# Tiles 4 to 7 of the first layernorm: from DMA transposes to TensorE transposes with the modulation in the eviction

## The chip, the core and the metric

One core of one Trainium2 chip runs the whole block. The metric is device time in microseconds (us); the kernel before takes 265.88 us (median of three runs, 265.82 to 266.1).

## The reference

S = 2048 rows (16 tiles of 128), D = 448, 16 heads of 28, window 256, bf16 data. Two sublayers follow each other, each with a layernorm, a modulation from the conditioning vector `c`, and a gated residual:

```python
mod = (silu(c) @ w_mod).reshape(..., 6, 1, -1)        # sa, ca, ga, sb, cb, gb
h = layernorm(x) * (1 + ca) + sa
q, k, v = split(h @ wqkv)                             # 16 heads of 28
p = softmax(where(0 <= i - j < 256, q k^T / sqrt(28), -1e9))
x = x + ga * (p v) @ wo
h = layernorm(x) * (1 + cb) + sb
z = gelu(h @ w_in);  z1 = z[:, :896];  z2 = layernorm(z[:, 896:])
x = x + gb * ((z1 * (w_sp @ z2 + b_sp)) @ w_out)      # w_sp is 2048 x 2048
```

## The kernel before

The program is a list of named operations with dependencies, tile rotations and one or more engines that may carry each of them. A stored string, `ORDER`, gives the sequence in which they are emitted: a number is an operation (in order of creation), `.1` picks its second engine, `/3` picks the buffer or PSUM bank. So every engine's queue is fixed in advance, and `Planner.emit` puts a semaphore wait ahead of an operation where one is needed. An engine that waits holds everything behind it in its own queue.

The names that matter here:

- `l1_t` (`ln_stats`, `ln_rs`): statistics of tile t's row on VectorE (DVE; `st` is L609, `ag` L612), `ve` = variance + eps (L616), `rs` = power -1/2 on GpSimd (POOL, L617), and `nm` = -mean*rs (L647, and L621 for the second layernorm, `l2`). `nm` lets the normalized tile `xn` be made as x*rs + nm on DVE, POOL (both L630) or ScalarE (ACT, L660); without it, L631 does (x - mean)*rs. `x2` is the same for the second layernorm.
- `transp_pe`: `tr` multiplies `xn` with an identity on TensorE (PE), and the eviction `hT` (L693 on ACT, L698 on DVE) applies the modulation from PSUM. Blocks 0, 1 and 2 (tiles 0, 1 and 2-3) go this way.
- `transp_dma`: `hx` is a DMA transpose of a tile from the SyncE (SP) queue (L717), and four `hm` operations (`modulate`, L707 or L710) apply the modulation in place for the block's 512 rows. Blocks 3, 4, 5 (tiles 4-7, 8-11, 12-15) go this way.
- `project`: `qk` and `v` matmuls, evicted by `qke` (L817 ACT, L820 DVE) and `ve<t>` (L834 ACT, L837 DVE). Four PSUM banks serve these matmuls from block 1 on.
- Attention by tile: `S`, `SE`, `SC`, `SL` are score matmuls, `E...` the exponentials (ACT, L887), `M...` the masks (POOL, L890), `PV`, then `oq` (L1058), `rec`, `nrm` (L1063), `oT` (L1067), `wo`, `x1` (L1077).
- Second half: `h2T`, `h2q`/`h2m` (transpose and modulation by tiles), `z1`/`z2` matmuls and gelus, the spatial matmuls `G` with `ga`/`gu`, the output matmuls `out` with `fin`. `wsp` are DMA transposes of `w_sp` from the SP queue. `wog` (L871) scales `wo` by the gate. `warm` are filler matmuls at the start.

PE runs in several shapes of its array: whole matmuls (mode 128), 32-row tiles for scores, 32-column tiles for `PV` and what is contiguous with it, and 64-row tiles for the ragged quarter of the contraction (`_r`).

Of the kernel before, what the change touches and what calls it, by code (L numbers as in the profile page):

```python
# [179 lines left out]
1 34 32 31 0 2 3 4 8 11 23 27 22 33 24 25 28 21 29 1693/0 1694 1695 1696 1697 1698 36 35 37/0 1699 1700 1701 15 67 38 1702 39 40/6 41 42 43 26 68 69  # L180
70 71/2 44 45 46 47 48 49 50 51 52 53 54 55 72/0 76/7 56 73 77.1 78/2 79.1 1703 74/4 1704 57.1 75 6 65.1 60.1 7 61.1 5 64.1 1705 1706 1707 1708 1709
12 18 10 9 62.2 125 126 127 63.2 58.2 180 182 128 129 181 95/7 96 85/0 90/1 91 80/2 105/3 81 86 115/6 106 97 98 82 87 88 92 93 99 83 89 94 116 107 117
118 119 108 109 130/2 133/4 134 131/7 183 66 184 1710 84.1 496/0,0 498/1 1711 1712 132.1 150/1 135/0 165/2 140/3 141 136 151 152 59.2 137 153 154 166
138 167 142 168 139 143 144 251 169 110/2 111 100/3 112 113 114 101 102 103 104 145/1 146 147 148 149 155/3 156 157 158 160/0 161 159 162 163 164
497/1,1 501/9 170/2 171 172 173 185 186 188.1/0 187.1/3 189/1 190 192/3 193 194 30.1 247 245 249 246 248 252 250 253 254 120/6 121 122 123 174.1
513/0,1 514/4 517/6 175/2 176 177 13 19 14 494/3 178 179 191.1 255 256/0 124.1 332 225/1 215/0 227 226 218 228 229 520/1,0 523/5 521/7 217 16 17 495
20 260 195/2 198 197 196 199.1 205/1 206 216 219.1 207 208 209.1 330 333 328 334 331 329 335 336 200/3 202 203 201 204 220/2 221 223 222 224 230/0 231
534/0,1 535/5 536/1 232 235/1 237 240/3 241 242 236 210/2 212 243.1 244 233.1 213.1 238.1 234.1 211 214 537/1,0 499 257.1/1 261 502 259.1/3 263
258.1/4 518 515 262 264 503/0 500 278/2 323/3 337 267 324 279 265 325 266 326 338 540 541 239.1 504/0 505 538 342.1/3 339.1/0 506.1/0 340.1/2 327 281
280 282 542/1,0 543/0 546/3 341.2/4 268/3 269 288/1 290 270 271 303/2 304 516/0 524 522 519 549/0,1 550/0 551/4 291.1 306.1 415 413 411 412 272.1 414  # L190
525/0 305 289 308/3 526 292.1 417 307.1 273/0 274 275 276 277 309 311 552/0,1 553 555 298/1 547/2 560/0 561 544/1 548 539 557 545 283/2 300 286 285
284 287 299 310 312 301 527/1 507/2 416 528/1 418 558 587/1,0 588/2 589/3 302.1 419 554 559 529/2 556 562 569/0 293/3 296 508/1 509 294 510 295 511
297 530 531 590/1,0 591 420 566/0 532 564 565 563 567 568 570 571/1 512 572/2 573/1 907 908 906 905 533 578/0 574 593 595/2,1 599/0 575 576 936 577
579 346 343 345 344 347.1 376/0 348.1 349.1 378 379 350.1 377 380.1 594 592 580.1/0 596/4 602/1,0 603/5 938 361/1 362 363 364 365.1 581/2 381/0 384
383 382 385.1 605/1,2 366/1 368 367 369 370.1 597/2 600/1 598 613/0 614 610 604/4 606 607 608 601 609 640/0,1 642/0 641/1 611 582/1 583 612 940 941
# [12 lines left out]
790/0 791 785/1 786 787 788 789 792/1 815/0 817/0,2 818 1433 1436 810 820 474/0 475 477 476 478.1 931/1 852/0,1 854/5 853/2 825/0 823 822 826 1035/2
1036 1037 793/1 935 794/3 795 934 819 824 821 827 834/0 796 797 798 835 932 933 1038 1043.1 970/0 971 974/2 972/1 973 855/0,1 858 856 1052/0 1053 1054
1069/3 1071 1039/2 1070 1040 1041 1072 1077.1 1042 1044 982 984 986 988 1055 1060.1 857 836.1/0 859 837/2 860/0,1 1090/3 1056/1 1091 1092 830/0 833  # L210
489/2 490 491 1057 1058 831 864/3 865/4 861/2 866 862/1 863 1093 1095.1 492.1 493.1 1059 1061.1 867/0,1 868/1 975 978.1 828 829 832 843/0 838/3 839
840 841 1086/1 1087 1088 842 987 985 989 983 990 991 869/3 1073/0 1074 1089 1076 1094.1 870/2,0 873 1430 1434 1438 871 1096/0 844 980 845/0 979 1075
846/2 1078 981.1 992 995/2 996 999.1/1 993.1/0 1000 994 1295/6 1305/7 1296 1307 1306 1300/3 1297 1301 1154/0 1150 1302 1330/1 1332 1333 1298 1303 1304
1153 1308 1309 1157 847/2 848 1005 1156 849 1155 850 851 1006 1007 1331 1151 1152 1103/1 1104 1158/2 872 874 879/0 1107/2 1340/7 876 880 875 878 877
1109 1097 1008 1009 887/0 1160 1335/4 1337 1110 1338 1343 1106 1334 1299 1079/1 997/2 888 1010 1011 1098 1080 1081 1159 998 1014/1 889.1/0 1015 1315/1
885/0 1105 1108 1112.1 1111.1 1336 1339 882 883 1317 1320/6 1012.2/0 1013 881 1316 1321 884 1310/0 1312 886 1453 1451 1441 1440 1445 1442 890/2 896/0
897 1082 1161 1162 898/0 1083 1120/0 1342 1124 1322 1325/3 1127 1318 1319 1313 1123 1323 1328 891/0 892 1341 893 894 895 1125 1290/1 1126 1326 1344
1324 1121 1122 1291 1311 1128/3 1002.2 1314 1004.1 1084 1163 1099 899/0 900/0 901 902 1292 1020 1001 903 904 1164 1085 1370/7 1180/0 1181 1327 1375/6
1371 1182 1003.2 1045/1 1329 1365/0 1376 1366 1184 1186 1185 1293 1294 1368 1373 1378 1187 1183 1188/2 1372 1367 1380/3 1350/1 1381 1369 1377 1374
1379 1382 1355/2 1199/0 1357 1195 1197 1285/0 1286 1356 1200 1165/1 1169 1172 1198 1383 1288 1353 1358 1202 1168 1170 1196 1201 1171 1021 1016 1022  # L220
1017.2 1100 1130 1023 1024 1129 1101 1025 1131 1026 1029.2/0 1384 1027.1/2 1102 1132 1133 1046 1047 1048 1049 1028 1134 1190 1189 1191 1359 1203/0
1167 1352 1287 1166 1345/3 1360/2 1214/0 1215 1210 1216 1212 1351 1173/3 1289 1354 1211 1361 1225/1 1229 1019.1 1050 1018.1 1348 1217 1363 1228 1051
1192 1205 1030 1455 1034.2 1213 1232 1218/1 1227 1362 1226 1032.1 1031.1 1385/0 1230 1347 1364 1033.1 1259/0 1193 1175 1204 1174 1219 1194 1176 1177
1220 1178 1179 1206 1221 1222 1207 1208 1223 1255 1346 1349 1231 1257 1260 1233/2 1386 1387 1395/2 1397 1390/3 1391 1135/1 1139 1062/3 1064 1235 1224
1209 1063 1065 1066 1388 1389 1142 1393 1138 1258 1262 1392 1394 1261 1256 1137 1405/1 1141 1410/0 1140 1136 1143/1 1412 1400/3 1401 1407 1396 1411
# [72 lines left out]
def bass_adaLN_cond__sliding_block__mixer_gmlp__prompt_kernel(  # L298
# [14 lines left out]
    FH = 896  # L313
# [300 lines left out]
    def ln_rs(name, prio, slot, t0, n, deps, nm):  # L614
# [4 lines left out]
        if not nm:  # L619
            return r  # L620
# [19 lines left out]
    def ln1(b, pr):  # L640
# [8 lines left out]
        for t in range(t0, t0 + n):  # L649
# [12 lines left out]
            if b:  # L662
                opts += [("pool", pool2_ns(512), f_p)] + ([("act", act_ns(512), f_a)])
# [640 lines left out]
```

## Time and profile before

| | |
|---|---|
| median of three runs | 265.88 us |
| profiled execution | 265.4 us, of which 263.7 us are the span from the first to the last instruction |
| granted TensorE clock | 1.000 |
| busy: PE, DVE, ACT, POOL | 257.2, 164.3, 128.8, 95.2 us |
| DMA transposes of `xn` and `x2` tiles | 28, issued from SP |
| mean busy share of the 16 DMA engines by q1 | 40.0% |

A row of a timeline gives start, length, engine, line, operation and tile, the count of instructions merged into it, and in brackets idle time of the engine with what ended it. A row of the chain of waits gives start, length and what. A row of windows gives for each engine busy time and count of instructions. A row of groups ends with busy time in total and the mean in ns, then the idle time before.

### The profile page before, as it was taken

What the parts mean: (1) busy time and instruction counts of PE and PEld (TensorE: products, weight loads), DVE (VectorE), ACT (ScalarE), POOL (GpSimd) and SP (SyncE); (2) the same over time, 40 slices, a digit from 0 to 9 for tenths busy, and PEclk for the clock granted to TensorE, in tenths of its full rate; (3) what the DMA queues carried; (4) which work ended last, traced back from release to release, by engine and by line L of the source; (5) the groups of instructions that cost most, each with busy time, mean ns of one, the idle gap of its engine ahead of it and who ended that gap; (6) DMA issues with size and microseconds to landing.
All of it is one profiled execution on the core that took longest, in us unless ns stands there. A gap on an engine that the chain in (4) does not pass through costs nothing.

```text
span 263.7 us, 7760 instructions
## 1 busy us (share of the span) xinstructions
PE 257.2 (98%) x3395; PEld 128.7 (49%) x3395; DVE 164.3 (62%) x387; ACT 128.8 (49%) x183; POOL 95.2 (36%) x148
## 2 busy tenths in 40 slices
PE   6999999999999999999999999999999999999996
PEld 2675455655455554543434444444444444444453
DVE  4798988788989997979587702352514213344453
ACT  4899999999999999778888000000000000000000
POOL 3594968878878776515331300000000000000000
DMA  6975560256994764768899400000000000000043
GB/s 225 357 193 120 145 163 5 62 125 145 227 114 118 118 87 101 85 130 154 144 199 222 92 2 0 0 0 2 0 0 0 2 0 0 0 2 17 0 142 119
DMA packets 61022, 23.86 MB, mean 91 GB/s; under 512 B 49854, under 2 KB 60861, under 8 KB 60989
## 3 DMA queue, kind: packets, MB, share of 16 engines
q1 hardware_dynamic: 60715, 22.92, 40.0%
q8 instruction: 26, 0.43, 0.6%
q10 hardware_dynamic: 274, 0.46, 0.5%
q14 instruction: 7, 0.06, 0.1%
HBM read 9.47 MB, written 1.84 MB: 43 GB/s over the span
## 4 chain that ended last, share of the span: by engine, by line
PE 91%; DVE 3%; POOL 2%; ACT 1%; DMA 1%; issue 1%; SPq 0%; DVEq 0%; POOLq 0%
PE ps L467 80%; PE ps L464 11%; DVE hT L707 1%; DMA hT<-xn 1%; ACT arena L887 1%; POOL xn L630 1%; POOL arena L890 0%; ACT WQK L734 0%; DVE x_sb L1077 0%; SPq L717 0%; DVE QKT L820 0%; ACT hT L693 0%; PE ps L779 0%; DVE xn L630 0%; DVE o_sb L1063 0%
## 5 line engine op out<-in xcount | busy, mean ns | idle before, releaser
L887 ACT ACTIVATE arena<-ps 128x1024 bf16<-128x1024 f32 x76 | 72.4, 1028 | 2.0 <-PE ps L467 1.4
L1212 DVE TENSOR_TENSOR tmpg<-ps,bsp_bc 128x512 bf16<-128x512 f32 x28 | 19.2, 689 | 60.2 <-PE ps L467 59.9
L467 PE MATMUL ps<-QKT,z 128*128 128x512 bf16 x224 | 52.1, 379 | 0.0
L890 POOL TENSOR_SCALAR_AFFINE_SELECT arena<-arena 128x512 f32<-128x512 f32 x60 | 39.1, 669 | 12.2 <-ACT arena L887 9.5
L467 PEld LDWEIGHTS ps<-QKT,z 128*128 128x128 bf16 x224 | 21.9, 98 | 26.4
L617 POOL TENSOR_TENSOR rs_all<-ve_all,neghalf 128x1 f32<-128x1 f32 (+2 forms) x27 | 18.9, 703 | 33.1 <-DVE ve_all L616 32.9
L467 PE MATMUL ps<-w_spD,z 128*128 128x512 bf16 x112 | 27.9, 379 | 0.0
L467 PE MATMUL ps<-w_spC,z 128*128 128x512 bf16 x112 | 27.8, 379 | 0.0
L467 PE MATMUL ps<-hT,w_in_sb 128*128 128x512 bf16 (+1 forms) x97 | 25.3, 380 | 0.0
L467 PE MATMUL ps<-w_in_sb,hT 128*128 128x448 bf16 (+1 forms) x102 | 24.6, 353 | 0.0
L467 PE MATMUL ps<-w_out_sb,z1T 128*128 128x448 bf16 (+2 forms) x119 | 22.0, 341 | 0.0
L609 DVE BATCH_NORM_STATS2 st_all<-z2raw 128x6 f32<-128x448 bf16 x32 | 18.7, 616 | 4.9 <-ACT z2raw L1135 3.9
L467 PE MATMUL ps<-hT,WQK 128*128 128x128 bf16 (+4 forms) x124 | 19.9, 291 | 0.1
L609 DVE BATCH_NORM_STATS2 st_all<-x_sb 128x6 f32<-128x448 bf16 x32 | 18.6, 608 | 0.0
L467 PE MATMUL ps<-QKT 28*64 28x64 bf16 (+3 forms) x944 | 17.7, 210 | 0.6 <-ACT arena L887 0.3
L1154 ACT ACTIVATE z1T<-ps 128x512 bf16<-128x512 f32 x28 | 15.9, 597 | 4.3 <-PE ps L467 4.2
L467 PE MATMUL ps<-arena,Vaug 128*32 128x128 bf16 x720 | 17.7, 221 | 0.0
L467 PEld LDWEIGHTS ps<-w_spC,z 128*128 128x128 bf16 x112 | 11.0, 98 | 13.2
L467 PEld LDWEIGHTS ps<-w_spD,z 128*128 128x128 bf16 x112 | 11.0, 98 | 13.0
L467 PEld LDWEIGHTS ps<-QKT 28*128 28x128 bf16 (+1 forms) x944 | 11.3, 97 | 11.7 <-ACT arena L887 5.9
L630 POOL TENSOR_SCALAR xn<-x_sb,rs_all,nm_all 128x512 bf16<-128x512 bf16 x20 | 15.4, 781 | 4.0 <-DVE nm_all L647 1.7
L467 PEld LDWEIGHTS ps<-w_out_sb,z1T 128*128 128x128 bf16 x119 | 11.6, 98 | 10.1
(93 smaller groups left out, 331.7 us busy)
## 6 DMA issues: line engine op xcount, KB each, us to landing
wmod_sb<-in_w_mod_dram SPq DMA_DIRECT2D x8, 224.0 KB, 3.8
w_in_sb<-in_B_w_in_dram SPq DMA_DIRECT2D x8, 224.0 KB, 4.0
out_dram<-fin SPq DMA_DIRECT2D x16, 112.0 KB, 1.7
x_sb<-in_A_x_dram SPq DMA_DIRECT2D x3, 448.0 KB, 8.1
bsp_bc<-in_B_b_sp_dram SPq DMA_DIRECT2D x1, 512.0 KB, 4.0
wqk_raw<-in_A_wqkv_dram SPq DMA_DIRECT2D x1, 452.0 KB, 5.7
wmod_sb<-in_w_mod_dram SPq DMA_DIRECT2D x1, 448.0 KB, 4.9
wmod_sb<-in_w_mod_dram ACTq DMA_DIRECT2D x1, 448.0 KB, 5.0
```

What stands on the lines that cost most here:

```text
L464: last = e.matmul(out_[32 * j:32 * j + 32], lhsT=lhsT[:, 32 * j:32 * j + 32], rhs=rhs, start=st, stop=sp, tile_position=(0, 32 * j), **kw)
L467: return e.matmul(out_, lhsT=lhsT, rhs=rhs, start=st, stop=sp, **kw)
L609: st = [dve("%sst%d" % (name, i), prio, dve_ns(D), lambda e, i=i, s_=s_: e.bn_stats(st_all[:, slot, t, i, :], s_()), deps, tens) for i, s_ ...
L617: r = pool(name + "rs", prio, 420 + 148 * n, lambda e: e.tensor_tensor(rs_all[:, slot, t0:t1], ve_all[:, slot, t0:t1], neghalf[:, t0:t1], ...
L630: return e.tensor_scalar(dst, src, rs_all[:, slot, t:t + 1], nm_all[:, slot, t:t + 1], ALU.mult, ALU.add)
L707: return e.tensor_scalar(hT[:, c_, cols], hT[:, c_, cols], modT[:, base_col + 4 + c_:base_col + 5 + c_], modT[:, base_col + c_:base_col + ...
L887: return P.op(name, pr, [("act", 925, lambda e: e.activation(e_out(), e_in(), ACT.Exp, scale=SCALE))], [s_op, t_exp0], tens + [pt], table= ...
L890: return pool(name, pr, pool_ns(n), lambda e: e.affine_select(out=pt32(slot_out.slot, off, dims), in_=pt32(slot_in.slot, off, dims), patte ...
L1154: g = P.op("z1g%d_%d" % (tb, ft), pr - 19, [("act", act_ns(512), lambda e: e.activation(z1T[:, ft, tb * 512:(tb + 1) * 512], ps[:, ten.slo ...
L1212: a = dve("ga%d_%d" % (tb, ft), pr, dve_ns(512), lambda e, tb=tb, ten=ten, tg=tg: e.tensor_tensor(tmpg[:, tg.slot, :], ps[:, ten.slot, :], ...
```

## The change

Block 3 is made by `transp_pe`, with one PSUM bank for each of the four 128-row chunks of h: `tr3_u_i` (chunk u, tile i) are 16 matmuls of 128 columns, and `hT3_u` are four evictions of 128x512 that modulate. The four `hx` and four `hm` of tiles 4 to 7 are gone. All ten `nm` operations are dropped and with them the ACT form of `xn` and `x2`; all normalizations use mean and rs. `ve` may run on POOL.

```diff
-    'by_pe': (1, 1, 1, 0, 0, 0),
+    'by_pe': (1, 1, 1, 1, 0, 0),
...
-    def ln_rs(name, prio, slot, t0, n, deps, nm):
+    def ln_rs(name, prio, slot, t0, n, deps):
         t1 = t0 + n
-        v = dve(name + "ve", prio, 75, lambda e: e.tensor_scalar(ve_all[:, slot, t0:t1], mv_all[:, slot, t0:t1, 1], EPS, None, ALU.add), deps)
-        r = pool(name + "rs", prio, 420 + 148 * n, lambda e: e.tensor_tensor(
+        def ve_fn(e):
+            return e.tensor_scalar(ve_all[:, slot, t0:t1], mv_all[:, slot, t0:t1, 1], EPS, None, ALU.add)
+        v = P.op(name + "ve", prio, [("dve", 75, ve_fn), ("pool", 110, ve_fn)], deps)
+        return pool(name + "rs", prio, 420 + 148 * n, lambda e: e.tensor_tensor(
             rs_all[:, slot, t0:t1], ve_all[:, slot, t0:t1], neghalf[:, t0:t1], ALU.pow), [v, t_nh])
-        if not nm:
-            return r
-        return dve(name + "nm", prio, 75, lambda e: e.scalar_tensor_tensor(
-            nm_all[:, slot, t0:t1], mv_all[:, slot, t0:t1, 0], -1.0, rs_all[:, slot, t0:t1], ALU.mult, ALU.mult), [r])
...
-    def norm(e, slot, t, dst, src, nm):
-        if nm:
-            return e.tensor_scalar(dst, src, rs_all[:, slot, t:t + 1], nm_all[:, slot, t:t + 1], ALU.mult, ALU.add)
+    def norm(e, slot, t, dst, src):
         return e.tensor_scalar(dst, src, mv_all[:, slot, t, 0:1], rs_all[:, slot, t:t + 1], ALU.subtract, ALU.mult)
...
-            opts = [("dve", dve4_ns(512), f_d)]
-            if b:
-                opts += [("pool", pool2_ns(512), f_p)] + ([("act", act_ns(512), f_a)])
+            def f_n(e, t=t, ten=ten):
+                return norm(e, 0, t, xnv(xn, ten.slot), spread(x_sb[:, t, :]))
+            opts = [("dve", dve4_ns(512), f_n)] + ([("pool", pool2_ns(512), f_n)] if b else [])
...
-        per = 1 if b == 0 and n == 1 else 2
+        per = 1 if b == 0 and n == 1 or n == 4 else 2
```

`ORDER` is new from end to end. Read by the names of the operations it stands for, it differs from the one before in this:

- Start. The loads of `wqk` come ahead of tiles 2-3 on SP, tiles 8-11 and `wmodG` ahead of `wo`. `xn1` goes from DVE to POOL; the statistics of tile 1 come ahead of one `hT0` eviction, those of tiles 2-3 behind three copies of `wqk`. `gateA` stands two `v` matmuls earlier.
- Tiles 4 to 7. `l1_4ve`, `l1_4rs`, then `xn6`, `xn5`, `xn4`, `xn7` stand on POOL behind `zv`, `M1_0`, `M0_0` and `M0_1` (before: `xn4` on DVE, the others between the masks). On PE, `tr3_0`, `tr3_1`, `tr3_3` stand between the last `qk2` matmuls and `SE2_1`, `tr3_2` after `v7_0`. `hT3_0`, `hT3_3`, `hT3_2` are on DVE, the last behind `oq0`; `hT3_1` is on ACT.
- Elsewhere. `nrm0`, `nrm3`, `nrm9`, `nrm14` go from POOL to DVE, `xn10`, `xn15`, `x2_12`, `x2_15` from ACT to POOL, `x2_3`, `x2_8`, `x2_11`, `x2_14` from DVE to POOL, `x2_1` and `xn2` from POOL to DVE, most `ve` of the layernorms to POOL. `x1_9` moves behind `oT10`. On SP, `wsp2_6`, which waits for all `PV`, stands ahead of `h2T13` and `h2T12`. The `G` and `out` groups come in another sequence with the same last tile.
- PE has 908 operations instead of 892, and changes its array shape 122 times instead of 117 (counted along the two orders).

More of the change, by code (lines that the diff above doesn't have):

```diff
@@ L184 @@
[L184 to L195, printed above, removed]
@@ L236 @@
[L236 to L238 removed]
+1 2 0 3 4 25 28 21 26 1695/0 1696 1697 1698 1699 1700 1701 32 36 35 34 67 68 69 15 31 22 27 70 37/2 1702 1703 1704 1705 71/0 74/1 33 38 40/3 41 42 43
+39 44 45 46 47 48 49 50 51 52 53 54 55 24 23 56 75.1 62.2 8 125 126 127.1 128 72/4 73 1706 1707 76/2 78/7 79 1708 1709 1710 77.1 63.1 6 60.1 7 5 11 58
@@ new lines @@
+575/0 572 574 571 573 570 585/0 580/1 581 602/2,1 582 943 944 583 584 600 601 606/0 607/1 428 384/0 386 385 387 388.1 586 587/1 603/4 604/2 608
+609/1,0 610/5 369/1 370 371 372 373.1 389/0 611/4 390 392 391 588/1 393.1 612/1,2 613 374/1 375 377 376 378.1 620/0 617 605 615 947 948 945 946 621
+647/0,1 618 589/1 590 591 614 592 619 327/3 329 364/2 366 593 616 622 629/0 328 365 367.1 330.1 649/1 648/0 430.1/3 1427 434 650/1,0 432.1/2 431.1/1
+429.1/4 433 435 368.1 331.1 630 631.1/1 653 651 654 929/0 404/1 405 406 930 407 408.1 931 932 933 655/2,0 656/3 934 935 949 936 937 950 951.1 652
@@ L239 @@
+1686/4 1678/1 1571 1567 1687 1513 1679 1680/4 1681 1682/7 1683 1688/7 1689 1690/5 1691/5 1692 1693 1694
 """
@@ L643, in ln1 @@
         if b == 0:
-            r = [ln_rs("l1_%d" % (t0 + i), pr, 0, t0 + i, 1, [ags[i]], False) for i in range(n)]
+            rs = [ln_rs("l1_%d" % (t0 + i), pr, 0, t0 + i, 1, [ags[i]]) for i in range(n)]
         else:
-            r = [ln_rs("l1_%d" % t0, pr, 0, t0, n, ags, False)]
-        rs = r if b == 0 else [dve("l1_%dnm" % t0, pr, 75, lambda e: e.scalar_tensor_tensor(
-            nm_all[:, 0, t0:t0 + n], mv_all[:, 0, t0:t0 + n, 0], -1.0, rs_all[:, 0, t0:t0 + n], ALU.mult, ALU.mult), r)] * n
+            rs = [ln_rs("l1_%d" % t0, pr, 0, t0, n, ags)] * n
         for t in range(t0, t0 + n):
@@ L651, in ln1 @@
             xn_ten[t] = ten
-            def f_d(e, t=t, ten=ten):
-                return norm(e, 0, t, xnv(xn, ten.slot), spread(x_sb[:, t, :]), False)
-            def f_p(e, t=t, ten=ten):
-                return norm(e, 0, t, xnv(xn, ten.slot), spread(x_sb[:, t, :]), True)
-            def f_a(e, t=t, ten=ten):
-                return e.activation(xnv(xn, ten.slot), spread(x_sb[:, t, :]), ACT.Identity, bias=nm_all[:, 0, t:t + 1], scale=rs_all[:, 0, t:t + 1])
-            opts = [("dve", dve4_ns(512), f_d)]
-            if b:
-                opts += [("pool", pool2_ns(512), f_p)] + ([("act", act_ns(512), f_a)])
+            def f_n(e, t=t, ten=ten):
+                return norm(e, 0, t, xnv(xn, ten.slot), spread(x_sb[:, t, :]))
+            opts = [("dve", dve4_ns(512), f_n)] + ([("pool", pool2_ns(512), f_n)] if b else [])
             xn_op[t] = P.op("xn%d" % t, pr + 0.1, opts, [rs[t - t0]], [ten], port=True)
@@ L1089, in bass_adaLN_cond__sliding_block__mixer_gmlp__prompt_kernel, with f_n @@
         ags = [ln_stats("l2_%d" % j, pr, 1, j, [lambda j=j: x_sb[:, j, :]], [x1_op[j]]) for j in js]
-        rs = ln_rs("l2_%d" % j0, pr, 1, j0, n, ags, True)
+        rs = ln_rs("l2_%d" % j0, pr, 1, j0, n, ags)
         for j in js:
             x2t = Ten(rot("x2", NX2))
-            x2 = P.op("x2_%d" % j, pr, [("pool", pool2_ns(512), lambda e, j=j, x2t=x2t: norm(e, 1, j, xnv(xn2, x2t.slot), spread(x_sb[:, j, :]), True)),
-                                        ("dve", dve4_ns(512), lambda e, j=j, x2t=x2t: norm(e, 1, j, xnv(xn2, x2t.slot), spread(x_sb[:, j, :]), True)),
-                                        ("act", act_ns(512), lambda e, j=j, x2t=x2t: e.activation(
-                                            xnv(xn2, x2t.slot), spread(x_sb[:, j, :]), ACT.Identity, bias=nm_all[:, 1, j:j + 1], scale=rs_all[:, 1, j:j + 1]))],
-                      [rs], [x2t], port=True)
+            def f_n(e, j=j, x2t=x2t):
+                return norm(e, 1, j, xnv(xn2, x2t.slot), spread(x_sb[:, j, :]))
+            x2 = P.op("x2_%d" % j, pr, [("pool", pool2_ns(512), f_n), ("dve", dve4_ns(512), f_n)], [rs], [x2t], port=True)
             h2_raw[j] = P.op("h2T%d" % j, pr, [("sp", 1250, lambda e, j=j, x2t=x2t: e.dma_start_transpose(
```

104 lines of the change are left out of this document (54 added, 50 removed).

## The prediction

> **What bounds the kernel now.** I read the page's busy line first, then the windows by stage, the chain of waits, and PE's timeline wherever the windows show it idle. The profiled execution took 265.4 us, 1.7 more than its span of 263.7 and 0.5 under the median of 265.88; I work out differences against that execution and add them to the median.
>
> ```profile
> PE 257.2 (98%) x3395; PEld 128.7 (49%) x3395; DVE 164.3 (62%) x387; ACT 128.8 (49%) x183; POOL 95.2 (36%) x148
> ```
>
> PE is busy for 98% of the span, no other engine for more than 62%. So the time is PE's own work plus the few holes in it, and an edit counts by what it does to one of these two. The windows (us of each engine, count in brackets, in the order PE, PEld, DVE, ACT, POOL, then granted clock, DMA share, GB/s) say where the holes are:
>
> ```profile
> 12.80:25.00 12.20, 12.20 (x184) 8.31 (x188) 10.96 (x30) 12.03 (x26) 8.71 (x12) 1.00 0.61 150
> 25.00:28.30 3.30, 2.80 (x112) 1.32 (x102) 3.11 (x8) 2.81 (x5) 1.95 (x3) 1.00 0.88 258
> 28.30:73.60 45.30, 45.30 (x1268) 25.18 (x1262) 38.92 (x84) 43.29 (x50) 37.16 (x53) 1.00 0.53 123
> 73.60:86.00 12.40, 11.77 (x370) 6.56 (x366) 11.06 (x27) 12.29 (x14) 10.24 (x15) 1.00 0.70 102
> ```
>
> From 12.8 to 86 us PE is idle in two places only: 0.50 us at 25 to 28.3 and 0.63 us at 73.6 to 86. The clock is granted in full, so none of this is throttling. The chain of waits (start, length, what) shows whose hole the first is:
>
> ```profile
> 12.78 5.91 PE ps L467 x84
> 18.68 1.50 POOL xn L630 x2
> 20.19 1.19 POOL arena L890 x2
> 21.38 0.94 SPq L717
> 22.36 2.60 DMA hT<-xn
> 25.16 1.74 DVE hT L707 x4
> ...
> 112.42 148.67 PE ps L467 x729
> ```
>
> For 8 us the chain leaves PE: POOL makes the normalized tiles 4 to 7, SP issues their DMA transposes, the last lands at about 25, and DVE modulates them in four operations of 1.74 us. That is the path the change replaces. It looks like 8 us to win; but PE had other work meanwhile (12.20 busy of 12.20 before 25). Only what PE actually waits for can be won. PE's timeline there:
>
> ```profile
> 24.81 0.44 PE L467 MATMUL ps<-arena,Vaug 128*32 128x128 bf16 x16
> 25.62 0.40 PE L464 MATMUL ps<-hT,WQK 128*32 128x512 bf16 x4 [0.37 <-DVE hT L707]
> 25.85 0.55 PE L464 MATMUL ps<-wv_sb,hT 128*32 128x448 bf16 x8
> 26.23 0.39 PE L464 MATMUL ps<-hT,WQK 128*32 128x512 bf16 x4
> 26.44 0.86 PE L464 MATMUL ps<-wv_sb,hT 128*32 128x448 bf16 x8
> 27.14 0.60 PE L464 MATMUL ps<-hT,WQK 128*32 128x512 bf16 x8
> ```
>
> Because matmuls are pipelined I count from start to start. The first wait for `hT` shows as 0.37 with DVE's L707 as releaser. The second is hidden in the counts: eight `v` matmuls take 0.38 (25.85 to 26.23) and then 0.70 (26.44 to 27.14), so 0.32 more. The last chunk's modulation was late for both. After 112.42 the chain is PE alone to the end, in one piece of 148.67 us, so nothing that is won or lost after that on another engine counts unless it opens a hole there.
>
> **PE's own work.** The change adds 16 transposes. The identity matmuls of the other blocks are in the trace:
>
> ```profile
> 15.35 0.61 PE L467 MATMUL ps<-ident,xn 128*128 128x128 bf16 x8
> 15.80 0.92 PE L467 MATMUL ps<-wv_sb,hT 128*128 128x448 bf16 x4
> ```
>
> Eight take 0.45 from start to the next start, 0.056 each: 16 cost **+0.9**. Their duration is longer, as the row of their group says (busy in total, mean ns of one):
>
> ```profile
> L467 PE MATMUL ps<-ident,xn 128*128 128x128 bf16 x16 | 1.5, 219 | 0.1
> ```
>
> 219 ns is the latency of one; eight of them in 0.45 us are pipelined, and PE's queue pays 0.056. The Trainium skill ("TensorE: Matmul & The Clock Gate", Part 4: PE-mode transpose) says otherwise of the price: about 275 ns for a 128x128 transpose in a kernel's context, dominated by access latency, with a copy out of PSUM after it; 16 of those would be 4.4 us. The trace's row has the latency near it, but shows that it overlaps; I go by the row, and take the other reading as rival C, in the row's own numbers.
>
> PE also changes its array shape 122 times instead of 117. A change's price comes from two stretches of the same kind, a run of `PV` and then a score shape:
>
> ```profile
> 46.04 0.53 PE L467 MATMUL ps<-arena,Vaug 128*32 128x128 bf16 x24
> 46.50 0.40 PE L467 MATMUL ps<-QKT 28*128 28x64 bf16 x16
> ```
>
> ```profile
> 80.06 0.87 PE L467 MATMUL ps<-arena,Vaug 128*32 128x128 bf16 x48
> 80.87 0.40 PE L467 MATMUL ps<-QKT 28*128 28x64 bf16 x16
> ```
>
> 24 take 0.46, 48 take 0.81: 0.0146 for one, and 0.11 left that does not grow with the count. Five changes: **+0.55** (between 0, if they hide in waits, and 0.55). The same 0.0146 prices the first hole above: 16 `PV` should take 0.23, and 24.81 to 25.62 is 0.81, so 0.58 lost; with the 0.32 the hole is 0.9.
>
> **The hole at 25.** With the transposes on PE, `hT3` comes straight from PSUM. The four SP issues (0.94 for the last), the 2.60 of the landing and the four in-place modulations leave the path; in their place stand `xn` on POOL as before, 0.9 of PE and four evictions, three on DVE, one on ACT. The path gets about 3 us shorter, and the wait goes: **-0.9**. What is late next is the evictions themselves. No row shows a 128x512 eviction with modulation; the nearest are these (busy, mean ns):
>
> ```profile
> L820 DVE CAST QKT<-ps 128x512 bf16<-128x512 f32 x18 | 12.3, 681 | 2.7 <-PE ps L464 2.0 <-PE ps L467 0.2
> ...
> L707 DVE TENSOR_SCALAR hT<-hT,modT 128x512 bf16<-128x512 bf16 x10 | 3.9, 429 | 0.5 <-DMA hT<-xn 0.5
> ...
> L1063 DVE TENSOR_TENSOR o_sb<-oq,rec_all 128x448 bf16<-128x448 f32 x9 | 6.7, 748 | 0.1
> ```
>
> I take 0.68, the cast from PSUM, not the 0.43 of the in-place form; a price of 0.43 would take 0.75 off rival B. The one eviction on ACT and the four `xn` on POOL leave those two engines about as loaded as they were.
>
> **The head.** Before, DVE normalizes tile 1 itself and then evicts `hT1`, for which PE's `qk1` waits until 12.78:
>
> ```profile
> 10.93 0.41 DVE L631 TENSOR_SCALAR xn<-x_sb,mv_all,rs_all 128x512 bf16<-128x512 bf16 x1
> 11.26 0.17 DVE L612 BATCH_NORM_AGGREGATE mv_all<-st_all 128x2 f32<-128x6 f32 x1
> ...
> 12.00 0.72 DVE L698 TENSOR_SCALAR hT<-ps,modT 128x128 bf16<-128x128 f32 x2
> ```
>
> In the new order `xn1` is POOL's, and of the 1.07 us between 10.93 and 12.00 only two aggregates of 0.17 stay ahead of the eviction. So 0.75 can go, if the statistics of tiles 2-3, which now stand ahead of it, do not wait for their load: I take **-0.75**, between 0 and -1.0. Part of it comes back. `wog` does not move with its queue, since it needs `wo`, whose load the new order puts later on SP:
>
> ```profile
> 18.60 2.00 DVE L871 TENSOR_TENSOR wo_sb<-wo_sb,ps 128x1792 bf16<-128x1792 bf16 x1
> 20.52 0.75 DVE L820 CAST QKT<-ps 128x256 bf16<-128x256 f32 x2
> ```
>
> Behind its 2.00 us stand the evictions `qke2` as before (0.75 for two); PE, arriving 0.75 earlier, finds the four `project` banks still full. I take **+0.3**, between 0 and 0.75.
>
> **The rest.** Ten `nm` go, most `ve` of the layernorms go to POOL, ACT loses four operations, `x1_9` moves behind `oT10`. In the 73.6 to 86 window this can relieve at most the 0.63 of holes; one of them is this wait for DVE:
>
> ```profile
> 85.56 0.94 PE L464 MATMUL ps<-wo_sb,oT 128*32 128x448 bf16 x16 [0.18 <-DVE oT L1067]
> ```
>
> I take **-0.3**, between +0.3 (another order has other small holes) and -0.6. `ve` on POOL has no row; it delays `rs` on the same queue by about what DVE's now takes, and what follows it (`xn` a stage ahead of its transposes) has slack, so nothing; without that slack, some 0.1 for each tile. The four `hx` leave SP's queue, and the loads and DMA transposes behind them start earlier; `wsp2_6` ahead of `h2T13` and `h2T12` holds these two until the last `PV`, and I cost that at nothing because PE then has the projections of earlier tiles to do. If this cover fails, a transpose of about 2.6 (the landing above) stands open. The new sequence of `G` and `out` has the same matmuls: nothing.
>
> **Sum.** +0.9 +0.55 -0.9 -0.75 +0.3 -0.3 = **-0.2**: 265.2 for an execution like the one profiled, **265.7** as median. By the skill's price for transposes (4.4 in place of 0.9) the sum would be +3.3.
>
> **The rivals.** *A, faster: the holes close and nothing comes back.* The head gives its whole 1.0, `wog` delays nobody, the 0.63 goes: 0.9 + 0.55 - 0.9 - 1.0 - 0.6 = -1.05, **264.8**. For it: DVE loses `nm` and the in-place `hm`, and the chain's 8 us detour disappears. Against it: DVE was 10.96 of 12.20 busy in just that stage.
>
> *B, slower: DVE becomes the bound between 13 and 28 us.* It has 1.24 + 0.19 = 1.43 us free there. Added are three evictions of 0.68, `nrm0` and `nrm3` of 0.75, `xn2` of 0.41: 3.95; four `hm` (1.74) and two `xn` of some 0.33 from start to start leave: 2.40. Net +1.55. DVE's free time is mostly waiting for PE's results, so not usable; where less than a tenth of it is, PE waits for banks for the whole 1.55 instead of the sum's 0.3, and the holes later stay as they are: -0.2 + 1.25 + 0.3 = +1.35, **267.2**. It decides when the `hT3` and `qke` evictions queue on DVE so that PE, in order, stands behind a full bank; the +0.9 and +0.55 on PE are then paid with nothing to set against them. For it: the windows. Against it: `nrm` has no early reader, and POOL and ACT share the evictions.
>
> *C, transposes at their latency.* If the 16 do not pipeline because each chunk waits for its tile, each costs 0.219 and not 0.056: +2.6, **268.3**. The eight in 0.45 us speak against it.
>
> *D, the replaced path did not matter.* If the wait at 25 goes to another producer (`E`, the scores' masks, `v`), 0.9 is not won, and the time is 266.6; this lies between the forecast and B, and I count it with B.
>
> **How the numbers follow.** A measurement of this kernel can tell about 0.2%, 0.5 us, from no change. Forecast 0.40, with its own range of 265.1 to 266.2, from 0.6 less (the rest's -0.6 and a smaller price of shape changes) to 0.5 more (the head's bound); A 0.27; B with D 0.29; C 0.04. Of the forecast 0.12 lies below 265.35 and 0.28 within 0.2%. Faster: 0.27 + 0.12 = 0.39. Slower: 0.29 + 0.04 = 0.33. Within: 0.28. The range goes from a little under A, 264.5, to B, 267.3; left out are C, and the ends of A and B where holes other than those costed open or close, together under 0.2.
>
> **What would show it.** Right: identity matmuls x32 in place of x16 in their group, 24 DMA transposes of `xn` and `x2` tiles in place of 28, `qk1` starting at about 12.0 in place of 12.78, no idle PE at 25 to 28 released by L707, and PE busy about 1.4 longer in total with 1.6 less of holes. B would show as idle PE at 18 to 30 released by L820, L698 or L871, with DVE over 95% in that window; C as identity matmuls apart from each other with idle time before them. I am wrong in kind if PE's busy time grows by more than 2, or if a hole of over 1 us stands after 30 us where none was before: then an order's later parts, which I cost at nothing, decide.

## The result and the profile after

The changed kernel takes 287.99 us (median of four runs, 287.62 to 288.92) against 265.88: 8.35% more, ratio 1.0835 with a 95% interval of 1.0806 to 1.0864. The forecast was 265.7, and its range ended at 267.3. Ratios further down are to runs of the kernel before taken beside each experiment (median 265.4 to 265.8), with a 95% interval in brackets. The busy line and the windows that answer to those of before:

```profile
PE 262.6 (92%) x3345; PEld 132.2 (46%) x3366; DVE 168.2 (59%) x363; ACT 126.8 (44%) x178; POOL 137.1 (48%) x167
```

```profile
12.80:25.00 12.20, 12.20 (x157) 8.76 (x157) 10.60 (x26) 11.48 (x24) 8.75 (x11) 0.87 0.68 163
25.00:28.30 3.30, 1.68 (x12) 0.70 (x10) 1.24 (x6) 1.52 (x3) 3.30 (x3) 1.00 0.01 2
28.30:73.60 45.30, 36.67 (x949) 20.24 (x953) 33.46 (x62) 31.99 (x37) 43.71 (x48) 0.92 0.24 48
73.60:86.00 12.40, 11.51 (x276) 6.33 (x274) 8.44 (x16) 9.10 (x10) 8.91 (x11) 0.86 0.49 117
```

Only one engine has become busier by much: POOL, from 95.2 to 137.1 us, and from 25 to 73.6 it works almost without a break (3.30 of 3.30, 43.71 of 45.30) while PE, DVE and ACT all have gaps. The number behind POOL's bracket is the granted clock: it fell to 0.86 to 0.92 in three of these stretches. PE is busy for 262.6 us, 5.0 more than with the same queue and a clock of 1.0 in the mult-add kernel below (257.6); how much of the 22 us the lower clock accounts for was not separated. Which work of POOL it is stands in the chain of waits:

```profile
22.05 1.02 POOL rs_all L618
23.17 8.26 POOL xn L626 x4
31.63 0.60 POOL arena L875
32.23 1.02 POOL rs_all L618
33.37 4.13 POOL xn L626 x2
37.50 1.24 POOL arena L875 x2
38.74 4.12 POOL xn L626 x2
42.85 1.24 POOL arena L875 x2
```

For 22 us without a break the chain is POOL, and most of it is `xn`: four tiles take 8.26 us. The chain of before had two of them in 1.50. PE's timeline shows what that does to the new transposes:

```profile
26.23 0.22 PE L466 MATMUL ps<-ident,xn 128*128 128x128 bf16 x1
27.37 0.23 PE L466 MATMUL ps<-ident,xn 128*128 128x128 bf16 x1 [0.93 <-POOL xn L626]
29.43 0.23 PE L466 MATMUL ps<-ident,xn 128*128 128x128 bf16 x1 [1.82 <-POOL xn L626]
31.48 0.29 PE L466 MATMUL ps<-ident,xn 128*128 128x128 bf16 x1 [1.82 <-POOL xn L626]
```

PE transposes a tile, then waits about 2 us for the next. The group rows of the normalization on POOL, after and then before (the last two numbers ahead of the bar's end are busy time and mean ns of one):

```profile
L626 POOL TENSOR_SCALAR xn<-x_sb,mv_all,rs_all 128x512 bf16<-128x512 bf16 x28 | 58.1, 2084 | 0.6
```

```profile
L630 POOL TENSOR_SCALAR xn<-x_sb,rs_all,nm_all 128x512 bf16<-128x512 bf16 x20 | 15.4, 781 | 4.0 <-DVE nm_all L647 1.7 <-DMA hT<-xn 1.3 <-DVE nm_all L621 1.0
```

Same engine, operation, shape and types; 2084 ns against 781. What differs is the arithmetic, x * rs + nm before and (x - mean) * rs after, and where one scalar comes from.

### The profile page after: what moved, and what is told of

Read it like the earlier page. It is cut to its first block, busy times and chain, and to the rows that moved or that the text cites. A ratio compares the mean times of both kernels' runs of the same rounds, so it can differ in the third digit from the quotient of the medians.

```text
span 285.7 us, 7668 instructions
## 1 busy us (share of the span) xinstructions
PE 262.6 (92%) x3345; PEld 132.2 (46%) x3366; DVE 168.2 (59%) x363; ACT 126.8 (44%) x178; POOL 137.1 (48%) x167
## 4 chain that ended last, share of the span: by engine, by line
PE 61%; POOL 20%; ACT 6%; DVE 5%; DMA 3%; issue 3%; SPq 0%; DVEq 0%; POOLq 0%
PE ps L466 57%; POOL xn L626 13%; ACT arena L872 5%; PE ps L463 4%; POOL arena L875 4%; DMA x_sb<-in_A_x_dram 2%; POOL rs_all L618 2%; DVE o_sb L1048 2%; DMA hT<-xn 1%; DVE st_all L608 1%; DVE x_sb L1062 1%; DVE z L626 1%; POOL ve_all L616 1%; POOL hT L692 1%; DVE hT L692 0%
## 5 line engine op out<-in xcount | busy, mean ns | idle before, releaser
L626 POOL TENSOR_SCALAR xn<-x_sb,mv_all,rs_all 128x512 bf16<-128x512 bf16 x28 | 58.1, 2084 | 0.6
L466 PE MATMUL ps<-w_in_sb,hT 128*128 128x448 bf16 (+1 forms) x109 | 26.5, 353 | 1.1 <-ACT z2raw L1118 0.5
L618 POOL TENSOR_TENSOR rs_all<-ve_all,neghalf 128x1 f32<-128x1 f32 (+2 forms) x27 | 19.8, 740 | 10.6 <-DVE ve_all L616 9.8
L466 PE MATMUL ps<-hT,w_in_sb 128*128 128x512 bf16 (+1 forms) x94 | 24.3, 380 | 0.2
L466 PE MATMUL ps<-w_out_sb,z1T 128*128 128x448 bf16 (+2 forms) x119 | 22.8, 341 | 0.0
L466 PE MATMUL ps<-arena,Vaug 128*32 128x128 bf16 x720 | 18.6, 229 | 1.7 <-POOL arena L875 1.0
L466 PE MATMUL ps<-QKT 28*64 28x64 bf16 (+3 forms) x944 | 18.5, 214 | 0.8 <-issue 0.8
L466 PEld LDWEIGHTS ps<-arena,Vaug 128*32 128x32 bf16 x720 | 14.2, 100 | 8.9 <-POOL arena L875 1.5
L463 PE MATMUL ps<-hT,WQK 128*32 128x512 bf16 x208 | 16.0, 395 | 2.2 <-DVE oq L1043 2.2
L1217 DVE TENSOR_TENSOR fin<-ps,x_sb 128x448 bf16<-128x448 f32 (+2 forms) x17 | 9.6, 593 | 12.9 <-PE ps L466 12.1
```

Of the source, the lines that this page charges most:

```text
L463: last = e.matmul(out_[32 * j:32 * j + 32], lhsT=lhsT[:, 32 * j:32 * j + 32], rhs=rhs, start=st, stop=sp, tile_position=(0, 32 * j), **kw)
L466: return e.matmul(out_, lhsT=lhsT, rhs=rhs, start=st, stop=sp, **kw)
L618: return pool(name + "rs", prio, 420 + 148 * n, lambda e: e.tensor_tensor(rs_all[:, slot, t0:t1], ve_all[:, slot, t0:t1], neghalf[:, t0:t1 ...
L626: return e.tensor_scalar(dst, src, mv_all[:, slot, t, 0:1], rs_all[:, slot, t:t + 1], ALU.subtract, ALU.mult)
L1217: fs.append(dve("fin%s%d" % (nm, t), pr, dve_ns(c1 - c0), lambda e, t=t, ten=ten, ft_=ft_, c0=c0, c1=c1: e.tensor_tensor(fin[:, ft_.slot, ...
```

## The experiments

**What makes POOL slow.** The first kernel changes nothing but the pair of operations on POOL.

```diff
         return e.tensor_scalar(dst, src, mv_all[:, slot, t, 0:1], rs_all[:, slot, t:t + 1], ALU.subtract, ALU.mult)
 
+    def norm_p(e, slot, t, dst, src):
+        return e.tensor_scalar(dst, src, rs_all[:, slot, t:t + 1], mv_all[:, slot, t, 0:1], ALU.mult, ALU.add)
+
...
-            opts = [("dve", dve4_ns(512), f_n)] + ([("pool", pool2_ns(512), f_n)] if b else [])
+            def f_p(e, t=t, ten=ten):
+                return norm_p(e, 0, t, xnv(xn, ten.slot), spread(x_sb[:, t, :]))
+            opts = [("dve", dve4_ns(512), f_n)] + ([("pool", pool2_ns(512), f_p)] if b else [])
```

`x2` gets its `f_p` in the same way.

> The changed kernel; only the arithmetic of xn and x2 on GpSimd is altered, from (x - mean) * rs to x * rs + mean: same operands in the other order, another pair of operations. (So the values differ from the reference's.) Order, waits and counts are those of the changed kernel. Theory S (the pair subtract, multiply is what GpSimd takes 2084 ns for): its 28 instructions fall to about 781 ns, the row of before, GpSimd's busy time falls by 28 x 1.3 = 36 us to about 101, and the time to 265.7, between 264.5 and 267.3, the prediction's own figures. Rival P (the operand, a mean read out of the interleaved statistics, or traffic with VectorE makes it slow): the 28 stay at about 2084 and the time at 288. Rival O (the new order is slow by itself): the 28 fall, and the time stays above 275.

Measured: 268.02 us, ratio to before 1.0088 (1.0065 to 1.0112), and the clock back at 1.0. That is 20 of the 22 us, but 0.7 above the range that was expected. Rival O is out as the cause of these 20 us, since this is the new order. The next keeps the operands where the change has them and replaces `ALU.subtract` by `ALU.add`; a third has `ALU.mult, ALU.subtract`.

> The changed kernel with (x + mean) * rs on GpSimd (values differ from the reference's): the scalars stand in the changed kernel's order, and only subtract has become add. If subtract alone is the slow part: 28 instructions at about 781 ns and the same time as with x * rs + mean, within 0.3%. If it is the order of the two steps, the multiplication last: 2084 ns and about 288 us.

> The changed kernel with x * rs - mean on GpSimd (values differ from the reference's): subtract, but as the second step. If any subtract on GpSimd is slow: 28 at about 2084 ns and 288 us. If only subtract as the first step is: 770 to 780 ns and 267.5 to 268.5 us.

Measured: 268.43 us (1.0118, 1.0067 to 1.0169) with add, 288.86 us (two runs; 1.0869, 1.0833 to 1.0904) with the subtract as second step. The group rows on POOL, in the order mult-add, add-mult, mult-subtract:

```profile
L629 POOL TENSOR_SCALAR xn<-x_sb,rs_all,mv_all 128x512 bf16<-128x512 bf16 x28 | 21.3, 770 | 0.6
```

```profile
L629 POOL TENSOR_SCALAR xn<-x_sb,mv_all,rs_all 128x512 bf16<-128x512 bf16 x28 | 21.4, 773 | 0.7
```

```profile
L629 POOL TENSOR_SCALAR xn<-x_sb,rs_all,mv_all 128x512 bf16<-128x512 bf16 x28 | 58.7, 2106 | 0.6
```

The mean out of the interleaved statistics is read in all three, so the operand (rival P) is not it; a subtract in either place is slow. The other way round, in the kernel before:

```diff
             def f_p(e, t=t, ten=ten):
-                return norm(e, 0, t, xnv(xn, ten.slot), spread(x_sb[:, t, :]), True)
+                return norm(e, 0, t, xnv(xn, ten.slot), spread(x_sb[:, t, :]), False)
...
-            x2 = P.op("x2_%d" % j, pr, [("pool", pool2_ns(512), lambda e, j=j, x2t=x2t: norm(e, 1, j, xnv(xn2, x2t.slot), spread(x_sb[:, j, :]), True)),
+            x2 = P.op("x2_%d" % j, pr, [("pool", pool2_ns(512), lambda e, j=j, x2t=x2t: norm(e, 1, j, xnv(xn2, x2t.slot), spread(x_sb[:, j, :]), False)),
```

> The kernel before with its 20 xn and x2 on GpSimd made as (x - mean) * rs in place of x * rs + nm; everything else as before, the nm operations stay. Theory S: the 20 go from 781 to about 2084 ns, GpSimd from 95 to 121 us busy, and the time rises by 8 to 20 us, to 274 to 286, since tiles 4 to 7 alone wait 3 x 1.3 = 4 us longer on the chain. Rivals P (as the operand) predicts the same here; rival O predicts no more than 268.

Measured: 285.88 us, ratio 1.0749 (1.0707 to 1.0792), the instruction at 2085 ns:

```profile
L631 POOL TENSOR_SCALAR xn<-x_sb,mv_all,rs_all 128x512 bf16<-128x512 bf16 x20 | 41.5, 2085 | 4.9 <-DMA hT<-xn 2.7 <-DVE nm_all L647 1.7 <-DVE nm_all L621 0.3
```

Block 3 still goes by DMA and the order is the old one, and with 20 slow instructions instead of 28 the loss is as large, 20 us. The same arithmetic on VectorE instead:

> The changed kernel, all 28 xn and x2 that its order gives to GpSimd put on VectorE at the same places, with the unchanged (x - mean) * rs. Theory S: VectorE makes them at 0.41 to 0.44 us each, 12 us more of work on an engine busy for 168 of 286; GpSimd falls to 79 us; most of the 22 us come back, 267 to 272, with VectorE as the new wait before 36 us (rival B of the prediction, made worse on purpose). Rival O: above 275.

Measured: 277.88 us (1.0448, 1.0415 to 1.0481), more than Theory S had said and above the 275 that was put down for rival O. The mult-add kernel, with the same order at 268.02, has already ruled that rival out, so the time is a miss of Theory S's estimate.

```profile
L596 DVE TENSOR_SCALAR xn<-x_sb,mv_all,rs_all 128x512 bf16<-128x512 bf16 x32 | 12.5, 419 | 1.2 <-POOL rs_all L588 1.2
```

The price of one, 0.42, was right: VectorE is five times as fast at a subtract as POOL. That some 11 us more of it cost 10 us of time against the mult-add kernel was not expected. PE loses 3.6 of 45.3 us from 28.3 to 73.6 and 3.9 of 57 from 86 to 143 (the mult-add kernel 1.4 and 1.0). That the added work stands in front of what PE waits for is the likely reason; it was not followed wait by wait. Last, the change with a form that POOL is quick at (the mended kernel in what follows):

```diff
         def ve_fn(e):
+            if slot < 2:
+                e.tensor_scalar(nm_all[:, slot, t0:t1], mv_all[:, slot, t0:t1, 0], -1.0, None, ALU.mult)
             return e.tensor_scalar(ve_all[:, slot, t0:t1], mv_all[:, slot, t0:t1, 1], EPS, None, ALU.add)
...
+    def norm_p(e, slot, t, dst, src):
+        return e.tensor_scalar(dst, src, nm_all[:, slot, t:t + 1], rs_all[:, slot, t:t + 1], ALU.add, ALU.mult)
```

> The changed kernel with the arithmetic of GpSimd mended and the reference's function kept: beside var + eps the same step also writes -mean (one small instruction more in 10 places, about 0.25 us each on GpSimd, 0.15 on VectorE), and GpSimd computes (x + (-mean)) * rs. Theory S: 28 xn and x2 at 0.77 us, time within 0.5% of the kernel with x * rs + mean (268.0), so 267.5 to 269: what the change is worth when its one slow instruction is taken out. It remains slower than before by 2 to 3 us.

Measured: 267.66 us, ratio 1.0087 (1.0053 to 1.0121), the instruction at 772 ns:

```profile
L632 POOL TENSOR_SCALAR xn<-x_sb,nm_all,rs_all 128x512 bf16<-128x512 bf16 x28 | 21.3, 772 | 0.7
```

So 20 of the 22 us are the subtract, and about 2.3 are left.

**The 2 us that are left.** In the kernels with mended arithmetic PE stops twice in the middle of an operation, where no wait can stand. From PE's timeline of the mult-add kernel:

```profile
64.80 0.88 PE L466 MATMUL ps<-arena,Vaug 128*32 128x128 bf16 x48
65.61 0.37 PE L466 MATMUL ps<-QKT 28*128 28x192 bf16 x11
66.77 0.28 PE L466 MATMUL ps<-QKT 28*128 28x192 bf16 x5 [0.79 <-issue]
...
85.44 0.51 PE L466 MATMUL ps<-arena,Vaug 128*32 128x128 bf16 x21
86.70 0.24 PE L466 MATMUL ps<-arena,Vaug 128*32 128x128 bf16 x3 [0.76 <-issue]
```

`SL8_0` is 16 matmuls without a wait; it does 11, stops for 0.79 us, and does 5. "Issue" means that nothing the profile shows was awaited. The changed kernel and its variants up to here all stop after the same matmul of `SL8_0`, and within one matmul of the same place in `PV11_d0`. I counted PE's instructions up to there: two for each matmul (weight load and matmul), one for each wait beyond an operation's first, 65 ahead of the first matmul (fitted to the first stop). The first matmul behind the two stops is then number 12.00 and 16.00 times 256. The page's queue of instruction fetches (q8) brings 16 KB at a time; its only packet near the first stop lies in the window from 64.2 to 65.3 us of the DMA view, ahead of which the data queue q1 had filled the engines (108.9% from 63.3 to 64.2, counting packets by their start):

```profile
q8 instruction: 1, 0.02, 5.8%
q1 hardware_dynamic: 30, 0.01, 4.1%
```

Theory F: PE holds one block beyond the one it works through, and runs dry when 256 instructions are used up before the next block is there. To move the boundaries without touching anything else, filler matmuls at the start are cut into pieces, with the same columns:

```diff
+        def w_fn(e, n_=n_, k_=((11, 11, 11, 11, 11, 11, 11, 11, 9, 9) + (1,) * 10)[i]):
+            for a_ in range(k_):
+                last = mm(e, ps[:, w_ten.slot, n_ * a_ // k_:n_ * (a_ + 1) // k_], warm[:, 0:128], warm[:, n_ * a_ // k_:n_ * (a_ + 1) // k_], True, True)
+            return last
```

> The kernel with x * rs + mean, and 96 more matmuls at the very start: ten filler matmuls of 512 columns are cut into 9 or 11 pieces each, so that everything behind them stands 192 instructions later in TensorE's instruction stream. Columns, order and waits are the same. Theory F (TensorE runs out of instructions where a block of 256 is used up in less than the about 3.4 us that the fetch of the next one takes: the stops of 1.03 and 0.98 us in the middle of SL8_0 and PV11_d0 fall on block boundaries): by the measured starts, shifted by 192, the shortest blocks take 3.3 instead of 2.4 us, the two stops go, and the time falls by 1.2 to 1.9 us, from 268.0 to 266.1 to 266.8. Rival W (the two stops are waits for data or for a bank): they stay where they are, and the time stays within 0.3 us or rises a little from the extra matmuls.

> The kernel before, with 44 more matmuls at the start (four filler matmuls of 512 columns cut into 12 pieces each): 88 instructions more in TensorE's stream ahead of everything else. Theory F: by the starts in its trace the two or three shortest blocks of 256 instructions shrink from 3.3 to about 2.1 to 3.1 us, so stops of 0.3 to 1.5 us in the middle of operations appear, in all 1.5 to 2.5 us: 267 to 268 against 265.4. Rival W: no such stops, and no more than 0.3 us of difference.

> The kernel before with 128 more matmuls at the start (its ten filler matmuls of 512 columns cut into 13 or 14 pieces): 256 instructions more, one whole block. Control to the kernel with 88 more. Theory F: the block boundaries fall on the same instructions as before, no stop in the middle of an operation, time within 0.4 us of before. Rival (the extra filler matmuls themselves cost): slower than the kernel with 88 more, which was 4.5 us behind.

> The changed kernel with (x + (-mean)) * rs on GpSimd, and 248 instructions more at the start. Theory F, by the starts of that kernel shifted by 248: the blocks that end in SL8_0 and PV11_d0 get 3.3 to 3.6 us instead of 2.4 and 3.3; the sum of what is missing to 3.7 us falls from 2.0 to 0.9. Time 266.2 to 267.2, against 267.7 without the shift. If the fetch starts late again because transfers are in its way (as it did with 192), 267.7 or more.

Measured: 268.86 us (1.0134, 1.0073 to 1.0195) with 192; the kernel before with 88 more 270.23 us (1.0161, 1.0124 to 1.0197), with 256 more 265.97 us (1.0014, 0.9998 to 1.0031); the mended kernel with 248 more 268.06 us (1.0087, 1.0062 to 1.0113). Only the time of the kernel with 256 more came as Theory F had said; 88 more cost about twice as much, and 192 and 248 more won nothing (for 248 that was the outcome put down for a late fetch). Where the stops went (the third column counts up to the first matmul behind the stop; the mended kernel's profiled execution took 269.27 us, 1.6 more than its median):

| kernel | operation | instruction / 256 | fetch, us | stop, us |
|---|---|---|---|---|
| mult-add | `SL8_0` | 12.00 | 64.24 to 65.27 | 65.74 to 66.77 |
| mult-add | `PV11_d0` | 16.00 | 83.56 to 85.20 | 85.72 to 86.70 |
| mended | `SL8_0` | 12.00 | 64.51 to 65.86 | 66.07 to 67.57 |
| mended | `PV11_d0` | 16.00 | 85.75 to 86.76 | 86.66 to 88.26 |
| mult-add, 192 more | `PV5_m1` | 10.00 | 52.55 to 53.84 | 54.73 to 55.23 |
| mult-add, 192 more | `SC8_0` | 12.00 | 62.68 to 63.83 | 64.27 to 65.47 |
| mult-add, 192 more | `PV11_m0` | 17.00 | 86.20 to 87.19 | 87.78 to 88.41 |
| before, 88 more | `SC4_0` | 7.00 | 40.32 to 41.27 | 41.83 to 42.64 |
| before, 88 more | last of `PV7` | 12.00 | 64.96 to 65.93 | 65.69 to 67.33 |
| before, 88 more | `SC12_0` | 16.00 | 84.70 to 85.81 | 86.18 to 87.21 |
| before, 256 more | `qk0_5_1` | 2.00 | 7.74 to 8.96 | 9.73 to 10.26 |
| before, 256 more | `PV1_3` | 5.00 | 28.45 to 29.38 | 30.04 to 30.76 |
| mended, 248 more | `SL8_0` | 13.00 | 64.44 to 65.39 | 65.53 to 66.94 |
| mended, 248 more | `wo9_3` | 17.00 | 84.61 to 85.49 | 85.88 to 87.07 |

```profile
65.28 0.64 PE L467 MATMUL ps<-arena,Vaug 128*32 128x128 bf16 x32
67.33 0.41 PE L467 MATMUL ps<-arena,Vaug 128*32 128x128 bf16 x16 [1.42 <-issue]
...
85.72 0.66 PE L467 MATMUL ps<-QKT 28*64 28x64 bf16 x59
87.21 0.23 PE L467 MATMUL ps<-QKT 28*64 28x64 bf16 x5 [0.82 <-issue]
```

These rows are of the kernel before with 88 instructions more: the kernel before has no stop of that kind by itself, gets three, and is 4.5 us slower. The three come to 3.5 us; its profiled execution is 5.4 behind, of which 1.1 arise in the last output matmuls and were not followed. With a whole block more the boundaries fall on the same instructions and the time is that of before. One thing there was not expected: that kernel has two stops, of 0.5 and 0.7 us, in the middle of operations. The one in `PV1_3` falls on a boundary that the kernel before crosses 1.9 us after the fetch has landed, at 28.32; here the fetch came a microsecond later. In the profiled executions PE ends 0.6 us later than before. Every stop of the table ends on a multiple of 256 and 1.2 to 1.7 us after the fetch has landed. That shows Theory F; rival W is out. What failed is my use of it: I had taken 3.4 us from one boundary to the arrival of the next block, and in these stops it is 2.9 to 5.1, since the fetch starts 0.6 to 2.7 us after the boundary. What delays the fetch was not tested; that data transfers are in its way is a guess. So with 192 and 248 more the stops moved (with 192 there are three, with 248 the two only became 1.41 and 1.19) and nothing was won. The Trainium skill ("Runtime: NRT & Kernel Launch", Instruction fetch mechanics) gives the blocks of 256 instructions and calls the crossing of a boundary mostly hidden. The block size agrees with the table; that the crossing is hidden does not hold for the stops of the table. It does hold for blocks as short where the fetch starts at once: the kernel before uses up two in 3.3 and 3.1 us without a stop, with the fetch 0.0 and 0.4 us after the boundary.

**The start.** In the mult-add kernel `qk1` starts at 13.57, not at the 12.0 that I had worked out.

VectorE's part of `ORDER`, read by names (`l1_1ve` and `l1_1rs`, on POOL, move along):

```diff
-  DVE: hT0_1  l1_1st0  l1_1ag  hT0_2  wqkf0_3
+  DVE: hT0_1  hT0_2  l1_1st0  l1_1ag  wqkf0_3
```

> The kernel with x * rs + mean; on VectorE the statistics of tile 1 (st, ag) go behind hT0_2 instead of ahead of it, as in the kernel before. Theory H (the late start of qk1, 13.57 against 12.78 before, comes from PE waiting at 9.4 for hT0_2 behind those statistics): the first qk0 matmuls start about 0.8 us earlier, qk1 at 12.8 to 13.2, and the time falls by 0.4 to 0.8 us to 267.2 to 267.6. Rival: xn1 on GpSimd then comes later by as much, hT1 waits for it, and nothing is won (within 0.3 us of 268.0).

Measured: 268.67 us (1.0101, 1.0078 to 1.0124), `qk0` at 9.43 and `qk1` at 13.58 as without the move, so Theory H falls. (The time is 0.6 more than without the move. This execution has a third stop, 0.4 us in `qk3_2_0`, at instruction 4.00 times 256; it ends 2.2 us after its fetch has landed.) The reason for the late start is in PE's fillers: the same ten, in the changed kernel and in the mult-add kernel (whose PE queues are the same):

```profile
5.27 1.14 PE L466 MATMUL ps<-warm 128*128 128x512 bf16 x4
...
7.49 0.60 PE L466 MATMUL ps<-warm 128*128 128x256 bf16 x4
```

```profile
5.27 1.68 PE L466 MATMUL ps<-warm 128*128 128x512 bf16 x4
...
8.45 1.06 PE L466 MATMUL ps<-warm 128*128 128x256 bf16 x4
```

In the second execution PE still ran at half rate at 8.45, 0.21 us for 256 columns from start to start; in the first it was at 0.11 by 7.49. The windows give the granted clock as 1.00 in both, so the half rate is read from the matmuls alone. The Trainium skill ("TensorE: Matmul & The Clock Gate", Part 1) says that the clock is raised after a busy window of about 3.4 us which runs freely, so at a time that varies from one execution to the next; the two rows agree that it varies. Executions of the new order where PE came to full rate earlier have `qk1` at 12.55 (add-mult) and 12.72 (mult-add with 192 more). They gain nothing by it. In the add-mult kernel PE waits at `gateA`:

```profile
17.91 0.92 PE L466 MATMUL ps<-wmod_sb,sc_sb 128*128 128x448 bf16 x4 [0.75 <-ACT arena L877]
```

The first transposes of tiles 4 to 7 start at 25.18 there, and at 25.20 in the mult-add kernel, whose `qk1` came a microsecond later.

**The hole of before**, tried from the other side: `hm3_1` of the kernel before on POOL; its token in `ORDER` gets the second engine.

```diff
-265
+265.1
```

> The kernel before; of the four in-place modulations of tiles 4 to 7 one, hm3_1, goes from VectorE to GpSimd, which idles then. VectorE has three instead of four behind the landing, so the last is done 0.44 us earlier. Of the hole of 0.9 us at 25 the second part, 0.32 at v7_1, goes: 265.3 against 265.6 for before; if the boundaries of the instruction blocks, which pass with 0.2 us to spare there, are then missed, the same or slower.

Measured: 265.71 us (1.0000, 0.9988 to 1.0013). Nothing won: PE's `qk3` began at 25.79 instead of 25.62, still released by VectorE; why that came later was not followed. None of the kernels measured here is faster than the kernel before.

## Why the prediction was wrong

- **The step that failed** is the sentence in "The hole at 25" that the eviction on ACT and the four `xn` on POOL leave these engines "about as loaded as they were", together with the term for the rest (-0.3), into which the ten dropped `nm` went without a price for the form that takes their place. I priced the normalization on POOL by the engine, not by the form. The diff says that its arithmetic becomes subtract, multiply; the trace of before has that form on DVE alone, never on POOL, so its price there was an unknown to be bounded, times 28. It is 1.30 us more for each, 36.5 us of POOL. The `nm` whose loss I had booked as a gain for DVE (rival A) was what kept POOL's form cheap.
- **A second thing was not in the sum at all**: stops at instruction blocks. They cost 1.9 us in the mult-add kernel's profiled execution and 3.1 in the mended one's; before has none.
- **Right, once the subtract is gone**: the hole at 25. In the mult-add kernel the window is full:

```profile
25.00:28.30 3.30, 3.30 (x81) 2.25 (x83) 3.01 (x5) 3.06 (x6) 3.30 (x7) 1.00 0.02 5
```

```profile
L466 PE MATMUL ps<-ident,xn 128*128 128x128 bf16 x32 | 3.7, 230 | 0.0
```

  The transposes stand without idle time before them, 230 ns each in duration but pipelined (eight of them 0.54 from start to start in the mended kernel, with a change of shape, where I had 0.45). Rival C is out, and the DMA transposes fell from 28 to 24 as said. The eviction that had no row, priced at 0.68, takes 0.79 to 0.81 on DVE.
- **The head's gain was given back whole, not by 0.3,** in the two executions with an early `qk1`. In one PE waits at `gateA` (above), in the other for `wog`, which starts at 19.65 there and at 18.60 in the kernel before:

```profile
21.73 1.28 PE L466 MATMUL ps<-hT,WQK 128*128 128x256 bf16 x9 [0.83 <-DVE wo_sb L861]
```

  That is of the kernel with 192 more, with `qk1` at 12.72. By these two the head term should have been 0. The mended kernel with 248 more, with `qk1` at 12.9, waits at neither and starts those transposes at 24.69, so it keeps half a microsecond of its earlier start.
- **Rival B named the wrong engine.** DVE did not become the bound: in the changed kernel it was busy for 1.24 of 3.30 us from 25 to 28.3. The place was right (PE waiting for what feeds the block of tiles 4 to 7), the mechanism not.
- **The sum for the mult-add kernel.** PE ends 2.3 us later than before. Where `SL8_0` begins, PE has done the same operations as before and the 16 transposes, and it is 1.0 behind (65.61 against 64.60). The two stops then cost 1.9 beyond the normal pitch, and some 0.6 comes back on the way to the end; which holes closed there was not taken apart. For the part up to `SL8_0` the prediction had 0.9 + 0.55 - 0.9 = 0.55 without the head; the other half microsecond stays open. The late start of `qk1` accounts for at most 0.3 of it: the add-mult kernel, with an early one, is 1.2 behind at `SL8_0`, the mended kernel with 248 more 0.7. Without the stops the change would cost about 0.4 us, close to the nothing that the prediction said of the parts that it saw; that kernel was not made, so this is argued, not shown.

## What to carry to other kernels

An instruction's price belongs to engine and arithmetic together: where a diff gives an engine a form that its trace does not show, bound it from far above and multiply by the count before anything else. When a matrix engine stops in the middle of an operation that waits for nothing, count instructions: if the stops lie on multiples of the fetch block, PE has used up a block before the next was there, and an edit that adds or removes instructions ahead of them moves the stops. Compare such edits with a control that shifts by a whole block, and look for stops in the control too.

## What the runs showed of the hardware

- A subtract in GpSimd's tensor-scalar instruction, as the first or the second step, takes 2084 to 2106 ns for 128x512 bf16; with add and multiply 770 to 781. On VectorE the subtract form takes 419.
- PE's instruction stream comes in blocks of 256. In the stops of the table PE went on 1.2 to 1.7 us after the fetch had landed (2.2 in one short stop elsewhere); the fetch itself took 0.9 to 1.6 us and started up to 2.7 us after the boundary. From 28 us on, blocks that PE used up in 2.1 to 3.8 us made it stop for 0.5 to 1.6 us there.
- 88 more instructions at the start, with the same columns to stream, cost the kernel before 1.6%; 256 more cost nothing that can be measured.
- In the three kernels with the subtract on POOL the mean granted clock fell to 0.97 to 0.99; with the subtract on VectorE it was 0.99 to 1.0. Why it fell was not followed: in the changed kernel it was 0.87 from 12.8 to 25, where PE was busy throughout, and 1.00 from 25 to 28.3, where it was not.
